# Fourier mixing and a squared-ReLU MLP: one class of transform rows split as 96 and 92 in place of 128 and 60

## The chip, the cores and the metric

The kernel runs on one core of one Trainium2 chip. The metric is the device time of one execution in microseconds (us), median over runs. For each run the granted clock of the matrix engine is recorded; all timed runs told here were in the fast state, but for the single run of one probe, whose state is unknown and whose time is not used. Engines are named as in the profile: PE is the matrix engine TensorE, PEld its weight loads, DVE VectorE, ACT ScalarE, POOL GpSimd, SP SyncE, which issues nearly all DMAs here.

## The reference

Eight sequences of 3008 rows and 256 columns go through a Fourier transform along both axes; the real part goes through an MLP with a squared ReLU.

```python
batch, seq, dim = (8, 3008, 256)
X = np.fft.fft(x, axis=1)
X = np.fft.fft(X, axis=2)
x = X.real.astype(np.float32).reshape(B * S, D)
h = x @ w_in                     # 256 -> 2048
r = np.maximum(h, 0.0)
return ((r * r) @ w_out).astype(np.float32)    # 2048 -> 256
```

All arithmetic of the kernel is fp32.

## The kernel before

The transform along the sequence is a matrix product. DVE folds the rows n, S-n, S/2-n and S/2+n, so that 753 rows remain; those are sorted into four classes, by n modulo 8, 4 and 2, and each class becomes tiles of at most 128 rows. These rows are the contraction of the matrix product, that is, the partitions of its operands.

```python
P = 128
R = 32
def class_tiles(S):
    half = S // 8 + 1
    tiles = []
    for c, order in enumerate((range(0, half, 4), range(2, half, 4),
                               range(1, half, 2), range(half, S // 4 + 1))):
        for r in range(0, len(order), P):
            tiles.append((c, order[r], order.step, len(order[r:r + P])))
    return tiles
```

For S = 3008 the tiles have 95 rows (class 0, n of 0 mod 8), 94 (class 1, n of 4 mod 8), 128 and 60 (class 2, n of 2 mod 4), and 128, 128 and 120 (class 3, odd n). Each table of cosines or sines is loaded by class; its source is cut in blocks of 128 rows, so that a tile can need several DMAs.

One output group (cosine or sine part, even or odd frequencies) is made of an "even" half, classes 0 to 2, and an "odd" half, class 3:

```python
def product(ps, c):
    ts = [t for t in range(NT) if TILES[t][0] == c]
    for t in ts:
        rows = TILES[t][3]
        w = we[t] if b is None else folded[b, t, which % 2]
        w = w[0:rows, kp]
        w = w[:, H:H + 1].to_broadcast([rows, n]) if which == 2 and b is not None else w[:, 0:n]
        nc.tensor.matmul(ps, w, tab[0:rows, kp, PLACE[t]:PLACE[t] + NC[kp][c]],
                         start=t == ts[0], stop=t == ts[-1])

def even_n():
    st["ps"] = psd.tile([P, 512], F32, name="pd", tag="d")[0:n]
    ...
    for c, at, nk in ((0, 0, n2), (1, n2, n2), (2, 2 * n2, n1)):
        product(st["ps"][:, at:at + nk], c)
```

The folded rows are the weights (128 or 127 columns), the table is the moving operand (94 or 95, and 188 or 189 columns here). The column E (d = 128) of sequences 1 to 7 is transformed for all seven at once, with weights of 7 columns (`b is None`). The groups of the next sequence are slipped one by one between the MLP steps of the current one, which are matmuls of 250 or 251 columns.

## Time and profile before

| | before |
|---|---|
| time, median of 3 runs | 1990.51 us (1989.71 to 1991.41) |
| span of the profiled run | 1991.9 us |
| PE busy | 98% of the span |
| DVE, POOL, ACT busy | 70%, 58%, 45% |
| PE on the chain that ended last | 94% |

The share of busy time says who is loaded; the chain that ended last says whose work set the end. Here both name PE. But an end of a matmul in the trace is modelled, and matmuls overlap in it, so PE can be "100% busy" and still lose time between two starts. That is why the prediction goes by the distance of starts, called steps below. An fp32 matmul has two records, called passes.

### The profile page before, as it was taken

Reading aid. Unit: us, or ns where it says so; the run is one execution under the profiler, and the core shown is the slowest. Engines: PE = TensorE matmul, PEld = TensorE weight load, DVE = VectorE, ACT = ScalarE, POOL = GpSimd, SP = SyncE. Lnnn points to the kernel's source line nnn. Section 1 sums busy time; section 2 is a strip of 40 time slices with the busy share of each in tenths; the row PEclk is TensorE's granted clock in tenths of the full one; section 3 lists DMA queues with packets and bytes.
Section 4 is the critical chain, followed back from the end, with each engine's and each line's share of the span. In section 5 each row is a group of like instructions: output and inputs, shape, how many; then the busy total and the mean of one; then the engine's idle time right before and its main releaser. Section 6 shows DMA issues by size and latency. Waiting matters only on the chain.

```text
span 1991.9 us, 27283 instructions
## 1 busy us (share of the span) xinstructions
PE 1957.8 (98%) x9104; PEld 1701.1 (85%) x9104; DVE 1391.3 (70%) x3492; ACT 896.2 (45%) x973; POOL 1158.8 (58%) x1695
## 2 busy tenths in 40 slices
PE   6999999999999999999999999999999999999998
PEld 3788888888888888888888888888888888888887
DVE  7889867776578765787558875677756876555554
ACT  1654444444444444444344443444444444445443
POOL 0037646666566655666557665666656675566664
PEclk8999999999999999999999999999999999999999
DMA  6331101110011111111011110121002100100100
GB/s 190 110 39 47 38 11 37 47 27 22 18 46 32 40 19 27 27 41 39 11 32 32 39 30 11 32 51 29 22 11 52 32 11 16 32 11 11 22 11 21
DMA packets 144687, 68.49 MB, mean 34 GB/s; under 512 B 128440, under 2 KB 135547, under 8 KB 144546
## 3 DMA queue, kind: packets, MB, share of 16 engines
q1 hardware_dynamic: 143470, 66.24, 14.1%
q8 instruction: 71, 1.16, 0.2%
q14 instruction: 70, 0.57, 0.1%
q10 hardware_dynamic: 1076, 0.52, 0.1%
HBM read 42.03 MB, written 24.68 MB: 33 GB/s over the span
## 4 chain that ended last, share of the span: by engine, by line
PE 94%; DVE 2%; DMA 1%; ACT 1%; SPq 0%; issue 0%; DVEq 0%; ACTq 0%
PE ph L412 16%; PE ph L413 16%; PE mA L465 16%; PE mC L465 16%; PE mB L465 16%; PE mD L465 8%; PE pd L349 5%; DMA xt<-in_x_dram 1%; DMA raw<-in_moe_w_in_dram 1%; DVE he L415 0%; DVE g L418 0%; ACT g L427 0%; ACT g L428 0%; SPq L163 0%; DVE g L417 0%
## 5 line engine op out<-in xcount | busy, mean ns | idle before, releaser
L427 ACT ACTIVATE g<-g 128x1004 f32<-128x1004 f32 (+1 forms) x384 | 399.6, 1041 | 894.3 <-DVE g L418 511.1
L415 DVE SCALAR_TENSOR_TENSOR he<-Et,gE,ph 128x251 f32<-128x251 f32 (+1 forms) x768 | 361.8, 471 | 476.6 <-PE ph L413 475.1
L435 POOL TENSOR_TENSOR s<-g 128x251 f32<-128x251 f32 (+1 forms) x376 | 248.9, 662 | 739.3 <-ACT g L428 668.1
L412 PE MATMUL ph<-Pt,G 128*128 128x251 f32 (+1 forms) x1536 | 453.4, 376 | 4.5 <-ACT G L237 3.4
L413 PE MATMUL ph<-Qt,G 127*128 127x251 f32 (+1 forms) x1536 | 451.3, 374 | 0.2 <-DVE Qt L362 0.2
L428 ACT ACTIVATE g<-g 128x1004 f32<-128x1004 f32 (+1 forms) x384 | 399.3, 1040 | 12.1
L465 PE MATMUL mC<-s,wsum 128*128 128x251 f32 (+1 forms) x1504 | 381.3, 374 | 0.0
L465 PE MATMUL mA<-g,wout 128*128 128x251 f32 (+1 forms) x1504 | 381.0, 375 | 0.0
L417 DVE TENSOR_TENSOR g<-he,ph 128x251 f32<-128x251 f32 (+1 forms) x768 | 320.6, 417 | 55.6 <-POOL s L437 0.5
L412 PEld LDWEIGHTS ph<-Pt,G 128*128 128x128 f32 x1536 | 287.2, 189 | 48.7 <-ACT G L237 4.0
L413 PEld LDWEIGHTS ph<-Qt,G 127*128 127x128 f32 x1536 | 291.1, 190 | 36.4 <-DVE Qt L362 0.6
L465 PEld LDWEIGHTS mA<-g,wout 128*128 128x128 f32 x1504 | 282.5, 189 | 41.7 <-issue 2.9
L465 PEld LDWEIGHTS mC<-s,wsum 128*128 128x128 f32 x1504 | 285.5, 190 | 34.5
L418 DVE TENSOR_TENSOR g<-he,ph 128x251 f32<-128x251 f32 (+1 forms) x768 | 314.2, 409 | 0.0
L436 POOL TENSOR_TENSOR s<-s,g 128x251 f32<-128x251 f32 (+1 forms) x376 | 282.0, 750 | 29.4
L437 POOL TENSOR_TENSOR s<-g 128x251 f32<-128x251 f32 (+1 forms) x376 | 291.4, 775 | 0.0
L438 POOL TENSOR_TENSOR s<-g,s 128x251 f32<-128x251 f32 (+1 forms) x376 | 246.0, 654 | 0.0
L465 PE MATMUL mB<-g,wsum 128*128 128x251 f32 (+1 forms) x752 | 220.5, 374 | 0.0
L465 PE MATMUL mD<-s,wout 128*128 128x251 f32 (+1 forms) x752 | 220.3, 374 | 0.0
L465 PE MATMUL mB<-s,wout 128*128 128x251 f32 (+1 forms) x752 | 219.9, 374 | 0.0
L465 PEld LDWEIGHTS mB<-g,wsum 128*128 128x128 f32 x752 | 142.6, 190 | 17.4
L465 PEld LDWEIGHTS mD<-s,wout 128*128 128x128 f32 x752 | 141.9, 189 | 17.7
(85 smaller groups left out, 1264.3 us busy)
## 6 DMA issues: line engine op xcount, KB each, us to landing
out_dram<-os SPq DMA_DIRECT2D x376, 56.0 KB
xt<-in_x_dram SPq DMA_DIRECT2D x24, 512.0 KB
xt<-in_x_dram SPq DMA_DIRECT2D x16, 384.0 KB
Et<-e_dram SPq DMA_DIRECT2D x7, 752.5 KB
out_dram<-os SPq DMA_DIRECT2D x288, 6.8 KB
raw<-in_moe_w_in_dram SPq DMA_DIRECT2D x16, 256.0 KB
raw<-in_moe_w_out_dram SPq DMA_DIRECT2D x16, 256.0 KB
xt<-in_x_dram SPq DMA_DIRECT2D x8, 480.0 KB
```

What stands on the lines that cost most here:

```text
L412: nc.tensor.matmul(hP, G1[:, fs], pt[:, ks], start=True, stop=True)
L413: nc.tensor.matmul(hQ, G2[:, fs], qt[:, ks], start=True, stop=True)
L415: nc.vector.scalar_tensor_tensor(out=t, in0=et[:, ks], scalar=gE[:, fc:fc + 1], in1=hP, op0=ALU.mult, op1=ALU.add)
L417: tt(out=g[:, h, 0, 0:n], in0=t, in1=hQ, op=ALU.add)
L418: tt(out=g[:, h, 1, 0:n][:, ::-1], in0=t, in1=hQ, op=ALU.subtract)
L427: act(v, v, AF.Relu)
L428: act(v, v, AF.Square)
L435: gt(out=s1, in0=g21, in1=g22, op=ALU.add)
L436: gt(out=s2, in0=s1, in1=g11, op=ALU.subtract)
L437: gt(out=s3, in0=g11, in1=g21, op=ALU.subtract)
L438: gt(out=s4, in0=g12, in1=s2, op=ALU.subtract)
L465: nc.tensor.matmul(acc[nm][:, i, 0:n], w, v[:, 0:n], start=j == 0 and i == 0, stop=j == NJ - 1, skip_group_check=True)
```

## The change

The intent is to split the 188 rows of class 2 evenly instead of filling the first tile: the tile count stays, the size is rounded up to a multiple of 32.

```diff
-        for r in range(0, len(order), P):
-            tiles.append((c, order[r], order.step, len(order[r:r + P])))
+        size = -(-len(order) // -(-len(order) // P) // R) * R
+        for r in range(0, len(order), size):
+            tiles.append((c, order[r], order.step, len(order[r:r + size])))
```

The classes of 95 and 94 rows stay one tile; class 3 stays 128, 128, 120.

## The prediction

> **What bounds the kernel now.** I read the stretches first, then the chain that ended last, then the records of one transform group. The busy time by stretch (columns: microseconds from the start, length, then busy time and instructions of PE, PEld, DVE, ACT, POOL, then the granted clock, DMA share and GB/s):
>
> ```profile
> 0.00:55.00 55.00, 35.09 (x102) 21.76 (x102) 41.91 (x117) 11.40 (x22) 0.70 (x6) 0.81 0.66 185
> 55.00:110.00 55.00, 50.23 (x249) 42.45 (x249) 48.43 (x104) 39.99 (x69) 0.00 (x0) 1.00 0.30 95
> 110.00:1976.00 1866.00, 1864.97 (x8720) 1630.68 (x8719) 1298.07 (x3265) 842.52 (x880) 1154.76 (x1684) 1.00 0.13 28
> ```
>
> From 110 us on, TensorE is busy 1864.97 of 1866 us at the full clock; DVE is busy 70% there, DMA 13%. The list of waits for this stretch has two waits of PE, 0.9 and 0.5 us. So here a nanosecond less between two matmuls is a nanosecond off the end, unless another engine runs out of slack. The first 55 us are different: PE is busy 35 of 55 us, the clock 0.81, the DMA share 0.66. The page's chain agrees with both:
>
> ```profile
> PE 94%; DVE 2%; DMA 1%; ACT 1%; SPq 0%; issue 0%; DVEq 0%; ACTq 0%
> ```
>
> But busy does not mean streaming without gaps, since the ends of matmuls are modelled. So I went by starts. Each fp32 matmul is two records, here called passes. Where the columns are 250 or 376 and nothing is in the way, passes start 0.212 and 0.316 us apart: 2N columns at 2.4 per ns, plus about 3 ns. One even group (rows n of 0 mod 8: 95; of 4 mod 8: 94; then of 2 mod 4, the class that the change touches: 128 and 60) in the timeline of weight loads, and of matmuls in narrow windows (columns: start, length, engine, line, operation, operands, rows*columns of the weights, moving operand):
>
> ```profile
> 1240.80 0.85 PEld L349 LDWEIGHTS pd<-sinT,wQ 95*127 95x127 f32 x6
> 1241.87 0.29 PEld L349 LDWEIGHTS pd<-sinT,wQ 60*127 60x127 f32 x2 [0.22 <-issue]
> 1242.38 0.30 PEld L412 LDWEIGHTS ph<-Pt,G 128*128 128x128 f32 x2 [0.22 <-issue]
> 1242.69 0.40 PEld L413 LDWEIGHTS ph<-Qt,G 127*128 127x128 f32 x2
> ...
> 1241.61 0.68 PE L349 MATMUL pd<-sinT,wQ 128*127 128x188 f32 x2
> 1241.87 0.58 PE L349 MATMUL pd<-sinT,wQ 60*127 60x188 f32 x2
> 1242.13 0.32 PE L349 MATMUL pd<-sinT,wQ 60*127 60x188 f32 x1
> 1242.38 0.69 PE L412 MATMUL ph<-Pt,G 128*128 128x250 f32 x2
> 1242.69 0.38 PE L412 MATMUL ph<-Pt,G 128*128 128x250 f32 x1
> 1242.91 0.38 PE L413 MATMUL ph<-Qt,G 127*128 127x250 f32 x1
> ```
>
> The reader is to see two holes. The weight loads of a 95-, 94- or 128-row tile run beside the matmul before (six in one unbroken piece). The load of the 60-row tile does not: the weight load path sits idle 0.22 us, then load and matmul start together. The same happens once more on the way back to 128 rows. No semaphore is blamed ("issue"): it is the array itself.
>
> **What the Trainium skill says.** "TensorEngine Tiling (Array Packing)", Available Configurations, has 64-row configurations for contractions of at most 64, and Key Properties says "Changing tiling mode (not just tile) drains the TensorE". The diff asks for no such mode; I infer that a 60-row operand gets it, because the holes stand at exactly 128 to 60 and 60 to 128, and not at 127 to 95, 95 to 94, 94 to 128 or 128 to 120. "TensorE: Matmul & The Clock Gate", LDWEIGHTS, says that a load costs by its columns and not by its rows, so 96 or 92 rows should load like 128; the trace agrees (187 to 191 ns for 128, 95 and 94 rows in this group). "FP8 and Floating Point Precision", TensorE Precision Notes, gives true FP32 four passes through the array: 4 times 250 columns at 2.4 per ns is 417 ns, and the trace has 0.424 for the two records together. "DMA: Bandwidth & Descriptors", Why a DMA increments its semaphore by 16 and not by 1, spreads a DMA over the largest k up to 16 that divides the slowest dimension; it bears on a column load below, and no figure of this trace isolates it.
>
> **The change part by part.** Only the 188-row class alters. One class has 95 rows and one 94 (one tile each before and after); the 376-row class gives ceil(376/3/32)*32 = 128, so 128, 128, 120 as before. The 188 rows become 96 and 92. The order of the instructions on PE, DVE, ACT and POOL is the same, and so is the number of passes: no work is removed, only the shape of two tiles.
>
> *Steady groups.* From the last 128-row pass to the second pass of the next operation, before: 1242.69 - 1241.61 = 1.08 us. After, if 96 and 92 rows run in the same mode as 128: three steps of 2*188/2.4 + 3 = 160 ns and one of 212 ns, 0.69 us. Saved: 0.39 us. Step by step: 0.26, 0.26, 0.25 and 0.31 in place of 0.16, 0.16, 0.16 and 0.21. The other groups show the same starts to 2 ns. How many are there after 110 us? The weight loads of line 349 count 28 of 60 rows for the cosine and 28 for the sine, two passes each: 28 groups. Two more with 7-column weights (the E column of the later sequences) have steps of 0.25, 0.16, 0.25 and 0.31 us: 0.28 us each to be saved. Sum: 28 * 0.39 + 2 * 0.28 = 11.5 us, all on the path.
>
> *Fold.* DVE instructions with 96 and 92 partitions in place of 128 and 60. In the startup the 60-row sum took 0.68 us and the 128-row one 0.68: nothing.
>
> *Loads of x.* 512 and 240 KB become twice 384 KB (92 is padded to 96). DMA share is 13% and loads run ahead: nothing. The 4-byte column loads of the 92-row tile divide by 4 and not by 15, so they may be slower; they are issued by 148 us and first read at 275 us: nothing.
>
> *Startup.* The source of the tables is cut in blocks of 128 rows, so the class takes four DMAs per table (64, 32, 32, 60 rows) in place of three (64, 64, 60). The chain runs here through the SyncE queue and the second weights:
>
> ```profile
> 26.39 0.61 SPq L163
> 27.04 0.57 SPq L163
> 27.66 0.61 SPq L163
> 28.31 0.91 SPq L163
> 29.34 0.57 SPq L201
> 29.95 6.71 DMA raw<-in_moe_w_in_dram
> 36.76 0.43 DVE fd L208
> 40.08 7.74 PE pd L349 x22
> ```
>
> A 64-row issue takes about 0.65 us with its gap, a 32-row issue 0.47 (measured with shorter rows), so each table costs 2*0.47 - 0.65 = 0.3 us more and the weights leave 0.6 us later. DVE waited 1.22 us for them at 36.76, so the delay passes through to 40.08. The piece of 22 passes there holds two even groups with 60 rows, worth 0.39 us each or 0.8. The other four groups of the first sequence fall before this, beside DMA waits. Startup: +0.6 - 0.8 = -0.2, an estimate with an uncertainty of about 1 us, because the clock there is still being granted.
>
> Sum: 1990.5 - 11.5 - 0.2 = 1978.8; I say 1979.0.
>
> **Rivals.** (1) The holes belong to every change of the row count, not to tiles of at most 64 rows. Then 96 and 92 keep them: about 1990. For: every change at 60 rows has them. Against: 127 to 95 starts 0.21 after a 250-column pass, as unbroken; 94 to 128 and 95 to 94 follow in 0.11, which the weight loads explain, and 128 to 120 in 0.315. (2) The time saved turns into a wait for DVE, which folds and joins in the same stretch: then perhaps half stays, 1985. Against: PE waits 1.4 us in 1866, and a group's saving of 0.39 us falls in a step of 4.67 us with DVE at 70%. (3) The startup takes more than estimated: the extra issue shifts which earlier DMA each of eight semaphores waits for, or the clock is granted later: 1980 to 1982. For: 18 to 30 us is issue by issue. Against: the waits for the last x tile and the last cosine tile fall on the same place in the sequence as before. (4) Both tiles full enough costs something new, say 92-row loads of E arriving late: one stall of microseconds, 1982 or so; 130 us of slack speak against it.
>
> **Range and chances.** The 11.5 us are counted from starts that agree to a few nanoseconds; if the mode is the cause, they vary by a few tenths. The startup adds 1 us either way and the run-to-run spread 0.9 us. Rival 1 has perhaps 7%, so 8 in 10 fit in 1977.0 to 1981.3. Two per cent is 39.8 us, more than three times all that the holes hold, and nothing in the change can cost as much: faster 0.01, same 0.98, slower 0.01.
>
> **What would show it.** In the changed profile, the load of the 92-row tile has no idle before it and starts beside the 96-row pass; the steps after the 96-row passes are 0.16 us; the piece of PE at one even group shrinks by 0.39 us. PE's idle after 110 us stays near 1 us, and the stretch from the first steady step to the end is 11.5 us shorter. The raw weights land about 0.6 us later than 36.66. I am wrong if the 92-row load shows the same 0.22 us, if PE waits for DVE grow by microseconds, or if the first 55 us change by more than 1.5 us.

## The result

| | before | changed |
|---|---|---|
| time, median of 6 runs | 1991.12 us (1989.71 to 1994.59) | 1981.58 us (1978.09 to 1982.1) |
| span of the profiled run | 1991.9 us | 1976.3 us |
| ratio | | 0.9945, 95% interval 0.9932 to 0.9958 |

A ratio here is the mean time of one kernel's runs over that of the other's of the same rounds, so not quite the ratio of the medians above (which is 0.9952). Both outputs are correct.

The stretches of the changed kernel, columns as in the prediction, show nothing of the gain in the steady stretch: it is as full as before, and only the span is shorter. (The clock of 1.00 in the first row is not to be trusted; see the last point of the closing list.)

```profile
0.00:55.00 55.00, 33.50 (x119) 22.96 (x119) 45.93 (x128) 12.60 (x24) 0.70 (x6) 1.00 0.65 185
55.00:110.00 55.00, 50.98 (x256) 43.80 (x256) 48.02 (x103) 41.96 (x72) 0.00 (x0) 1.00 0.33 101
110.00:1960.00 1850.00, 1848.99 (x8696) 1627.61 (x8694) 1294.17 (x3257) 838.77 (x876) 1152.37 (x1684) 1.00 0.13 28
```

PE was busy all but 1.03 of 1866 us before, and is busy all but 1.01 of 1850 us now. The holes were inside "busy". The same even group as in the prediction shows them gone, first in the timeline of weight loads, then of matmuls in narrow windows:

```profile
1228.71 1.17 PEld L350 LDWEIGHTS pd<-sinT,wQ 95*127 95x127 f32 x8
1229.85 0.35 PEld L413 LDWEIGHTS ph<-Pt,G 128*128 128x128 f32 x2
1230.22 0.40 PEld L414 LDWEIGHTS ph<-Qt,G 127*128 127x128 f32 x2
...
1229.52 0.48 PE L350 MATMUL pd<-sinT,wQ 96*127 96x188 f32 x2
1229.68 0.48 PE L350 MATMUL pd<-sinT,wQ 92*127 92x188 f32 x2
1230.00 0.38 PE L413 MATMUL ph<-Pt,G 128*128 128x250 f32 x1
1230.22 0.37 PE L413 MATMUL ph<-Pt,G 128*128 128x250 f32 x1
```

All eight loads are one piece with no idle before it, and so is the way back to line 413. From the second 96-row pass (1229.52) to the second pass of line 413 it takes 0.70 us, where before it took 1.08.

The two traces have the same 9104 passes in the same order, so each pass can be set against its twin. Relative to the kernel before, the changed one is ahead by 4.89 us at the first pass of the MLP, by 4.68 us less than 1 us later, still by 4.56 us at 206 us, and by 15.57 us at the last pass. From 206 us on, every one of the 28 even groups of sequences 1 to 7 adds 0.384 to 0.387 us, the two E groups add 0.09 us each, and the odd groups add nothing: 11.0 us in all (10.99 summed). So the steady part gained 11.0 us, and these two profiles differ by another 4.6 us that arose before it. That second part is not all the change's: six passes of the startup, which are the same in both kernels, read as follows in the timeline of PE (before, then after):

```profile
40.08 4.13 PE L349 MATMUL pd<-cosT,wP 128*128 128x376 f32 x6 [2.88 <-DVE Et L366]
```

```profile
38.63 2.16 PE L350 MATMUL pd<-cosT,wP 128*128 128x376 f32 x6 [2.03 <-DVE Et L367]
```

The profiled run of the kernel before had only half the clock there, and the changed one all of it. The chain of the changed kernel's startup, answering to the one in the prediction (start, length, engine and line):

```profile
26.59 0.43 SPq L164
27.07 0.57 SPq L164
27.68 0.61 SPq L164
28.34 0.91 SPq L164
29.37 0.57 SPq L202
29.98 5.26 DMA raw<-in_moe_w_in_dram
...
35.33 0.43 DVE fd L209
...
38.63 2.37 PE pd L350 x8
```

The second weights are issued at 29.37 us against 29.34 before, not 0.6 us later, and in this run they landed 1.4 us earlier.

### The profile page after: what moved, and what is told of

It is laid out like the page before. It is cut to its first block, busy times and chain, and to the rows that moved or that the text cites. A ratio compares the mean times of both kernels' runs of the same rounds, so it can differ in the third digit from the quotient of the medians.

```text
span 1976.3 us, 27286 instructions
## 1 busy us (share of the span) xinstructions
PE 1941.4 (98%) x9104; PEld 1701.0 (86%) x9104; DVE 1391.0 (70%) x3492; ACT 896.0 (45%) x973; POOL 1156.4 (59%) x1695
## 4 chain that ended last, share of the span: by engine, by line
PE 93%; DVE 3%; DMA 1%; ACT 1%; SPq 0%; issue 0%; DVEq 0%
PE ph L413 16%; PE ph L414 16%; PE mC L466 16%; PE mA L466 16%; PE mB L466 16%; PE mD L466 8%; PE pd L350 5%; DMA xt<-in_x_dram 1%; DMA raw<-in_moe_w_in_dram 0%; DVE he L416 0%; DVE g L419 0%; ACT g L428 0%; ACT g L429 0%; SPq L164 0%; DVE g L418 0%
```

## The experiments

My theory after the result: a matmul whose weights have at most 64 rows runs in another mode of the array, each change of mode costs about 0.19 us in steady state, and nothing else of the change matters. Rivals: the gain comes from the even split or the different transfers; any change of the row count costs; a large part comes from the startup. Eleven kernels ran, all correct. Beside the times I give, for each profiled run, the time from the first MLP matmul to the end of the span ("rest"): it leaves the startup out. It was 1937.34 us before and 1926.63 us for the changed kernel.

### The startup with filler matmuls, in both kernels

```diff
+    warm = psm.tile([P, 2, CH], F32, name="warm", tag="mD")
+    def fill(count):
+        for _ in range(count):
+            nc.tensor.matmul(warm[:, 0, 0:P], ident, ident, start=True, stop=True, skip_group_check=True)
...
+    fill(22)   # before the first loads of x; then 6, 3, 8 and 8 before later waits of PE
```

> The kernel before with 47 idle-time matmuls of 128 columns (identity times identity, result unused) put into the waits of TensorE in the first 50 us, so that its clock is granted early and stays. Theory (scatter of the runs and part of the gap between the two profiles is the startup's clock): startup reaches the first L412 pass near 51 us, not 54.5, and the runs fall together within 1 us at 1987 to 1989, 2 to 4 us under the plain kernel before. Rival (the startup is bound by transfers and DVE alone): no change, 1990 to 1992, or slower by the filler.

> The same filler matmuls in the changed kernel. Theory: the distance to the filled kernel before is what the change itself is worth with the clock out of the way: 11.0 us in the steady part (28 groups of 0.386 and two of 0.09, as the two traces show) and 0 to 1 us in the startup, so 1976 to 1978 and a ratio to the plain kernel before of 0.992 to 0.993. Rival (the startup gained by the change itself, 4 us): the distance between the two filled kernels is 14 us or more.

Measured on one chip, 5 runs each: filled before 1990.47 us (1989.62 to 1990.82), ratio to plain before 0.9988 (0.9975 to 1.0001); filled changed 1979.78 us (1978.89 to 1980.23), ratio 0.9935 (0.9923 to 0.9948). The plain kernel before was at 1992.32 us (1991.24 to 1994.33) in the same rounds.

The distance of the two filled kernels is 10.7 us. Their rests are 1937.57 and 1926.63 us, 10.94 apart; in the profiled pair the changed kernel reached its first MLP matmul 1.1 us later than its partner. So a startup gain of 4 us through the change falls, at least with the fillers in. The plain runs say the same: the ratio 0.9945 of 1991.1 us is 11.0 us (8.4 to 13.5 by its interval), no more than the steady part alone. The fillers did not do what I meant: the clock was granted at 5 us but dropped to half again at 11.9 us in the filled kernel before, and was only there to stay from 32.4 us. Both medians missed what I expected (1987 to 1989 and 1976 to 1978). The runs of these two scatter less (1.2 and 1.3 us in five runs against 3.1 in nine of the plain kernel), but a third filled kernel, told last, scattered by 2.8 us against 2.4 of its unfilled partner, so that fillers lessen the scatter is not shown. Nor is it shown that they make the kernel faster, since the interval reaches 1.

### The split of before, the small tile filled up with zero rows

```diff
+    USED = [96 if rows == 60 else rows for _, _, _, rows in TILES]
+    for tab in (cosT, sinT):
+        nc.gpsimd.memset(tab[0:96, :, PLACE[3]:PLACE[3] + NC[0][2]], 0.0)
...
-                    rows = TILES[t][3]
+                    rows = USED[t]
```

Loads and folds of x use the same count; the tables are loaded as before, over zeros.

> The split stays 128 and 60, with the table loads of the kernel before, but the 60-row tile is computed over 96 rows, the last 36 times zeros in the tables. Theory (a matmul of at most 64 rows changes the mode of the array, and nothing else of the change matters): every steady group is 0.386 us shorter than before and the E groups 0.09, exactly as in the changed kernel, in all 11.0 us less, 1979 to 1982. Rival A (an even split or the other transfers bring the gain): no gain, 1990 to 1992. Rival B (any change of the row count costs): 128 to 96 to 128 keeps the holes, 1990 to 1992.

Measured: 1979.77 us (1977.72 to 1983.61), ratio 0.9937 (0.9923 to 0.9951). Rest 1926.58 us. Set against the trace of the changed kernel, every one of the 30 even groups takes the same time to 2 ns. The even split and the table loads have no part in the gain, and 128 to 96 to 128 costs nothing: rivals A and B fall. (The loads of x for the small tile did grow here; the pair of kernels with an added matmul, below, changes no load at all.) More work (36 rows of zeros) is faster than less.

### Mode changes by themselves

```diff
+    for first, second in (((128, 128), (128, 128)), ((128, 128), (60, 128)), ((60, 128), (60, 128)),
+                          ...
+        for step in range(8):
+            rows, cols = second if step % 2 else first
+            nc.tensor.matmul(pr[0:cols, 0:188], G1[0:rows, 0:cols], cosT[0:rows, 0, PLACE[4]:PLACE[4] + 188],
+                             start=True, stop=True, skip_group_check=True)
```

> The changed kernel with 13 blocks of 8 matmuls of 188 columns behind its end, weights in turn of 128 and 60, 60 and 60, 128 and 96, 128 and 65, 128 and 64, 128 and 32, 64 and 32 rows, then 128 and 65, 128 and 64, 128 and 7, 7 and 7 columns. One matmul is two passes; unbroken it takes 0.32 us. Theory: 128 with 96 or 65 rows, and 60 with 60, are unbroken at 0.32; 128 with 60, 64 or 32 rows cost about 0.19 us more at each change, 0.51 per matmul; 64 with 32 rows cost it too; columns do the same: 65 unbroken, 64 and 7 in turn with 128 broken, 7 and 7 unbroken. Rival (any change of size drains): 96 and 65 break as well. Rival (a small matmul is slow in itself): 60 with 60 takes 0.51 too. The time of the whole is about 45 us longer and means nothing.

Measured, as steps in ns from one pass to the next, read from the starts in the trace (a typical cycle of each block; the closing block repeats the first, at 159, and is left out):

```
weights in turn            step into  inside  step back  inside
                           the second second  to first   first
128 and 128 rows              159      159       159       159
 60 and  60 rows              159      159       159       159
128 and  96 rows              159      161       159       161
128 and  65 rows              159      161       159       161
128 and  64 rows              253      263       249       263
128 and  60 rows              253      263       249       263
128 and  32 rows              252      264       247       263
 64 and  32 rows (half clock) 446      473       447       474
128 and  65 columns (half)    313      313       313       314
128 and  64 columns           252      210       253       263
128 and   7 columns           253      162       253       263
  7 and   7 columns           159      159       159       159
```

The second step is longer because the first pass of a mode is recorded with the start of its weight load. So one change costs 94 ns before it plus an exposed weight load, 104 ns for 128 columns, 51 for 64 and about 2 for 7: 198 ns for full columns. The border is exactly between 64 and 65, for rows and for columns. It is not the only one: 64 and 32 rows in turn are broken too, so there is another between 32 and 64 rows, whose place was not looked for. A small matmul is not slow in itself: 60 with 60 rows runs unbroken. From the last three steps of the block of 32 rows on, the clock was at half until the end of the block of 65 columns; 313 ns is the unbroken step at half clock, so 65 columns are unbroken and 64 with 32 rows are broken. The time of the whole, 2019.65 us, means nothing.

### 124 and 64 rows, 123 and 65 rows

```diff
-        size = -(-len(order) // -(-len(order) // P) // R) * R
+        size = 124 if c == 2 else P        # and 123 in the other kernel
```

> The 188 rows split as 124 and 64. Theory (64 rows or fewer change the mode): the steady groups keep all four long steps of the kernel before, 0.25, 0.26, 0.25 and 0.31 us, and the time is that of before, ratio 0.998 to 1.002. Rival (what counts is how even the split is, or that the tile is nearly empty): something between, 0.997 or less.

> One row moved: 123 and 65. Theory: no long step is left, each group is 0.386 us shorter than with 124 and 64 although 65 rows use hardly more of the array; the ratio to before is 0.993 to 0.996, that of 96 and 92. Rival (evenness): as 124 and 64.

Measured on one chip, 4 runs each, the kernel before at 1992.6 us: 124 and 64 took 1991.93 us, ratio 1.0 (0.9985 to 1.0015); 123 and 65 took 1981.02 us, ratio 0.9945 (0.993 to 0.996). One row makes 10.9 us. The weight loads of the same group, first with 64 rows, then with 65:

```profile
1238.59 0.85 PEld L350 LDWEIGHTS pd<-sinT,wQ 95*127 95x127 f32 x6
1239.66 0.29 PEld L350 LDWEIGHTS pd<-sinT,wQ 64*127 64x127 f32 x2 [0.22 <-issue]
1240.17 0.30 PEld L413 LDWEIGHTS ph<-Pt,G 128*128 128x128 f32 x2 [0.22 <-issue]
```

```profile
1232.14 1.17 PEld L350 LDWEIGHTS pd<-sinT,wQ 95*127 95x127 f32 x8
1233.28 0.35 PEld L413 LDWEIGHTS ph<-Pt,G 128*128 128x128 f32 x2
```

The rests are 1937.58 and 1926.61 us: group by group those of the kernel before and of the changed kernel. How even the split is does not matter.

### The mode change put back into the changed kernel

```diff
                 for c, at, nk in ((0, 0, n2), (1, n2, n2), (2, 2 * n2, n1)):
+                    if c == 2 and b is not None:
+                        w = folded[b, 1, which % 2][0:60, kp]      # 0:92 in the control
+                        w = w[:, H:H + 1].to_broadcast([60, n]) if which == 2 else w[:, 0:n]
+                        nc.tensor.matmul(st["ps"][:, 448:449], w, tab[0:60, kp, PLACE[1]:PLACE[1] + 1],
+                                         start=True, stop=True)
```

> The changed kernel with one more matmul of a single column in each of the 34 even groups, between the classes, its weights cut to 60 rows (unused result). This puts the mode change back without touching split, loads or folds. Theory: two more holes per group, about 0.39 us, besides what the two passes take for their weight loads, about 0.2 us: some 0.6 us times 28, 16 to 18 us more than the changed kernel, ratio to before 1.002 to 1.004. Rival (the holes belong to the 60-row tile's data or buffers): only the 0.2 us of the passes.

> The control: the same added matmul with weights of 92 rows. Theory: only the two passes, about 0.2 us times 28, 5 to 7 us more than the changed kernel, ratio to before 0.997 to 0.998; the difference to the 60-row one is 0.39 us per group. Rival: the two added-matmul kernels are alike.

Measured, 4 runs each: with 60 rows 1995.28 us, ratio 1.0021 (1.0006 to 1.0036); with 92 rows 1987.87 us, ratio 0.9976 (0.996 to 0.9993). The 60-row matmul makes the changed kernel slower than the kernel before, the control does not. The difference per group was smaller than expected: the traces give 0.253 us and not 0.39, the added passes 0.222 us as expected, and rests of 1939.91 and 1932.72 us. The weight loads show where it lies (60 rows, then 92):

```profile
1241.49 0.62 PEld L350 LDWEIGHTS pd<-sinT,wQ 95*127 95x127 f32 x4
1242.21 0.29 PEld L360 LDWEIGHTS pd<-sinT,wQ 60*127 60x127 f32 x2
1242.52 0.62 PEld L350 LDWEIGHTS pd<-sinT,wQ 96*127 96x127 f32 x4
```

```profile
1237.26 0.62 PEld L350 LDWEIGHTS pd<-sinT,wQ 95*127 95x127 f32 x4
1237.81 0.30 PEld L360 LDWEIGHTS pd<-sinT,wQ 92*127 92x127 f32 x2
1238.03 0.62 PEld L350 LDWEIGHTS pd<-sinT,wQ 96*127 96x127 f32 x4
```

Passes of one column are over before the next weight load is (0.111 us per pass in the control), so the load is exposed in the control already; only the remainder of the hole is left as a difference. This reading fits the loads shown, but no run tests it by itself. My expectation took over the size of a hole between passes that are long enough to hide a load.

### The E column's weights 72 wide

The E groups gained only 0.09 us each. By the measured border for columns, their 7-column weights are a mode of their own. The seven small tiles become one, and the weights are read 72 columns wide:

```diff
+    WE = const.tile([P, 2 * NT * NE + 72], F32, name="WE")
...
-                    w = we[t] if b is None else folded[b, t, which % 2]
-                    w = w[0:rows, kp]
+                    at = (2 * t + kp) * NE
+                    w = WE[0:rows, at:at + nw] if b is None else folded[b, t, which % 2][0:rows, kp]
```

> The changed kernel itself, once more on a third chip, as the partner of the next two. Theory (steady part 11.0 us, startup between 1 us lost and 4 us gained by the luck of the clock): ratio 0.993 to 0.996. Nothing but the first 55 us should differ from the first profile of it by more than 0.2 us.

> The changed kernel with the E column's weights read 72 columns wide in place of 7 (the other columns are neighbours in the same tile; their results are not used). Theory (64 columns or fewer are a mode as well; a change costs 0.09 us of drain and a weight load that no longer hides): in the E groups of the changed kernel three long steps remain, 0.30, 0.25 and 0.31 us; they go, 0.29 us for each of the four places, 1.1 us in all; the time is 0.5 to 1.5 us under the changed kernel, which 5 rounds may not tell, but the trace does. Rival (the long steps there belong to the rows of the 92-row tile or to the short moving operand): they stay.

> Both at once: 72 columns and the filler matmuls in the startup. Theory: 1.1 us under the filled changed kernel, 1978 to 1980, scatter about 1 us, the fastest median of all. Rival: the fillers gain nothing beyond less scatter, and it is as the wide one.

Measured on one chip, 5 runs each, the kernel before at 1991.62 us: the changed kernel 1981.46 us, ratio 0.9952 (0.9939 to 0.9966); 72 wide 1980.79 us, 0.9947 (0.9935 to 0.996); 72 wide with the fillers 1979.56 us, 0.9941 (0.9929 to 0.9954). The intervals overlap, so the times do not tell the three apart, and the 1.1 us that I expected between the two filled kernels is not seen (1979.56 against 1979.78 us, on different chips). The traces do: of the E even group in the changed kernel and in the wide one,

```profile
280.20 0.75 PEld L350 LDWEIGHTS pd<-cosT,we 95*7 95x7 f32 x8 [0.32 <-issue]
281.27 0.30 PEld L413 LDWEIGHTS ph<-Pt,G 128*128 128x128 f32 x2 [0.32 <-DVE he L416]
```

```profile
283.42 0.35 PEld L353 LDWEIGHTS pd<-cosT,WE 95*72 95x72 f32 x2
284.04 0.69 PEld L353 LDWEIGHTS pd<-cosT,WE 94*72 94x72 f32 x6 [0.27 <-DVE WE L286]
284.75 0.35 PEld L418 LDWEIGHTS ph<-Pt,G 128*128 128x128 f32 x2
```

The holes at both ends are gone (the name in the bracket on the way back is only the last event before the end of the wait). In their place the first group waits 0.27 us once for DVE, since all weights now lie in one tile and the loads of the second tile wait for the last fold. Of 1.1 us expected, the trace shows 0.85 (from 0.63 us behind to 0.22 ahead of the same pass in the changed kernel's repeat). The changed kernel's own repeat had a rest of 1926.51 us, 0.12 us from the first profile, while its startup was 3.1 us longer.

## Why the prediction was right or wrong

**The bound.** Right. PE set the end in the steady part before and after, and a hole removed there came off the end in full. PE waits for DVE did not grow: its two waits are 0.9 and 0.5 us in both traces.

**The mode.** Right in its effect, and this is now shown rather than inferred: 60 rows filled up to 96, one row moved from 64 to 65, and the alternation at the end each tell it apart from the rivals. Rival 1 (every change of row count) and rival 2 (a wait for DVE) have no part. That what changes at the border is the tiling mode of the skill's page is the name that fits; no run reads the mode itself, nor whether the array or the program's encoding picks it.

**Steady groups.** 28 times 0.39 us was predicted and 28 times 0.386 measured, 10.8 us.

**The E groups.** The mis-sized term: "Two more with 7-column weights ... 0.28 us each to be saved" turned out as 0.09. I put all their long steps down to the 60 rows. Two of the three, those on the way back to the MLP, belong to the change from 7 to 128 columns and stay. A 7-column weight load exposes 2 ns, so leaving the 128-row mode for the 60-row mode had cost only its 94 ns. The steady sum is 11.0 us and not 11.5.

**Fold and loads of x.** Nothing was predicted and nothing seen; the steady groups of the zero-filled kernel, with other loads, are the same to 2 ns.

**Startup.** The step of the table loads failed: "each table costs 2*0.47 - 0.65 = 0.3 us more". From the first issue after the last wait of the sine table (25.76 us, before 25.74) to the second weights it took 3.61 us with six issues and 3.60 with five, because two 32-row issues replaced one of 64 rows and the 60-row issue was shorter as well (0.43 us against 0.61 in length). Nothing left 0.6 us later. The rest of the startup, put at -0.2 with 1 us of uncertainty, was too narrow: in single profiles, the first MLP matmul started at 54.49 and 52.08 us with holes (128 and 60; 124 and 64), and at 49.60, 52.68, 51.33 and 53.14 us without (the changed kernel twice, zero-filled, 123 and 65). The change's own share of this is not settled to better than a microsecond or so. In the first pair of profiles the startup gained nearly 5 us, which is more than the 1.5 us that I had named as a sign of being wrong; the filled pair leaves a loss of 0.2 us or so (10.7 of the times less 10.94 of the rests). That my sum for the startup was near nothing as well is luck: its +0.6 did not come, and its -0.8 was not measured by itself.

**The time.** The predicted time was 1979.0 us; the median of six runs was 1981.58, 0.3 us above the upper end of my range, and two of the six were below 1979. It lies where rival 3 would have put it (1980 to 1982), but the later table loads that rival 3 supposed are not in the profiled run, which is the fastest of the six. The four slower runs have no profile; their mean clock was lower (0.995 to 0.998 against 0.999 in the two below 1979). The kernel before does the same in the later rounds: its five runs at 0.999 took 1989.1 to 1990.7 us, the twenty others 1990.0 to 1994.3. So the scatter goes with the recorded clock in both kernels, and nothing shows that the change causes it. The kernel before, from whose earlier median I subtracted, was 0.6 us slower in its six runs; the ratio 0.9945 on the earlier 1990.51 us would be 1979.6. What the change saves, 11.0 us in the steady part, is what the prediction said within 0.5 us; what I understated is the scatter of the startup.

## What to carry to other kernels

Where PE is the bound, look at the steps between starts and at idle in the weight load track before a tile of another size: a profile that calls PE 100% busy can hold such holes. Keep the rows and the columns of all weights in a stream above 64, by an even split or by zero rows, or put the small ones side by side so that they share one pair of changes; 36 rows of zeros were cheaper here than their absence. Small weights among themselves are safe only where they were measured: 60 with 60 rows and 7 with 7 columns ran unbroken, 64 with 32 rows did not. And measure a gain of half a per cent by aligning two traces pass by pass behind the startup, since the startup alone scatters by about a third of it (49.60 to 53.14 us in the kernels without holes).

## What the Trainium skill lacked or had wrong

- "TensorEngine Tiling (Array Packing)", Key Properties, says that a mode change drains and gives no cost. Measured here: 94 ns, and besides it the weight load that no longer hides, 104 ns for 128 columns, 51 for 64, 2 for 7, at the full clock and with fp32 passes of 188 columns.
- The same page, Available Configurations, does not say that a plain matmul gets a mode by its size alone. Here the size alone brought the cost of a change: 64 rows break the stream and 65 do not (1991.93 against 1981.02 us); for columns the probe shows the same border.
- The same page, When to Use Tiling, recommends row tiling for contractions of at most 64 and names no cost for one small tile in a stream of large ones. Here such a tile, alone and not packed with others, lost 0.386 us per group with full-width weights; packing was not tried.
- "TensorE: Matmul & The Clock Gate", LDWEIGHTS, ties the cost of a load to columns and not to rows. The records agree for 128, 95 and 94 rows (187 to 191 ns in the group shown), and the loads exposed in the probe go with the columns too; the page doesn't say that a load stops overlapping when the mode changes, which is 0.22 us of idle in the load track here.
- On reading the clock, beyond a general caution about clock records in "TensorE: Matmul & The Clock Gate", no page says that a profile can show the full clock before its first record: the stretch from 0 to 55 us of the changed kernel reads 1.00 with the first record at 26.9 us, while its first passes of 256 columns start 0.427 us apart, about twice the 0.215 that unbroken ones of the same size take from 53 us on.
